# A new order for a list-scheduled kernel: the planner's table of priorities found anew with other costs for transfers and a few operations

## The chip, the core and the metric

The kernel runs on one core of a Trainium2 chip. Its engines are TensorE (PE, matrix products), VectorE (DVE), ScalarE (ACT), GpSimd (POOL) and SyncE (SP, which only issues transfers here). Each has a queue of its own and works through it in order; semaphores make one wait for another. The metric is the device time of one execution in microseconds, less is better.

## What is computed

Three layers one after the other, for 4 sequences of 576 tokens. Masks, scales and the subtraction of the maximum are as usual.

```python
# 1: attention, 8 heads of 64, each token sees itself and the 63 before it
scores = where(0 <= rel < 64, q @ k.T / 8, -1e9)
x = softmax(scores) @ v                              # heads side by side: 4 x 576 x 512
# 2: gated MLP over tokens
h = maximum(x @ w_in, 0)                             # 512 -> 1024
u, v = h[..., :512], h[..., 512:]
v_n = (v - mean(v)) / sqrt(var(v) + 1e-6)
v_s = einsum('ts,bsd->btd', w_spatial, v_n) + b_spatial[None, :, None]
y = (u * v_s) @ w_out
# 3: four causal attention heads of 64, each token's output is mixed from its top 2
logits = y @ w_gate
out = sum over e of gate_e * (softmax(causal(q_e @ k_e.T / 8)) @ v_e @ wo_e)
```

## The kernel before

Every product is made in three passes (high x high, high x low, low x high part of each number), so most operands exist as a pair of tiles with names in h and l: `xh, xl`, `vh, vl`, `wsp_h, wsp_l`, `woh, wol`, and weights as two tiles that both read `w`. Making a pair is a copy (`copy`, L432 on ACT, L434 on POOL, L436 on DVE) and a subtraction (`sub`, L445). Matmuls are issued by one helper (L421), transposes on PE at L688. In rows, `bank` is one of 8 PSUM banks.

Of the first layer, `a_couple` handles a pair of tiles of heads: the score products (`kt,qa`, 24 matmuls of 128 columns, called a score run here), the masked maximum on DVE (L654), the exponential on ACT (L660), the normalisation (`s_norm`, on ACT, DVE or POOL: L666, L669, L672), transposes on PE (`ident,pa`), the product with v (`pt,wol`), and then the pair `xh, xl`, and `xt` for the last 64 tokens. Of the second, `b_v` makes a v product for 128 tokens (`w,xh` and `w,xl`, 12 matmuls of 512 columns; the short one for the last 64 tokens reads `w,xt`), `b_u` a u product (`xh,w`, 12 of 288), `b_mix` the spatial product with its gate, and `prep64` unpacks and splits a weight that came by a load. w_out is multiplied into the weights of the third layer (`fold`, reading `w,woh`, 12 matmuls of 256). Of the third, `c_split` makes the pair of y for one of four column groups, `c_qk` and `c_v` are its products, `c_vt` that for the last 64 tokens of two sequences together (`w,zt`); `zeros` clears tiles (`pg`, L1107) that live from then on in the space that the second layer frees.

None of this runs in the order in which it is written. Each step is a node with the engines that may do it and a cost on each; the class `Planner` keeps, while the program is built, a clock of its own for each engine, and at each free engine starts the ready node with the lowest number in the table `KEY` (one number a node), given room in the ring of tiles that it needs. Scalars weigh in: `SWITCH` (the price of a change between kinds of matmul on PE), `DVE_BIAS`, `POOL_BIAS` and `EFT` (which of several possible engines takes a node), each with a value for each of two phases. The second phase begins with the third layer's tiles. `start` is where a node's end is worked out, with a model of the transfers that SP issues (`LAT`, `ISSUE`, `WAY`, `RATE`, `FLIGHT`, `BEHIND`). Costs and models change no instruction; they change the order and the engine. While operands are awaited at the start, up to 68 dummy products (`bank<-ident`, fillers) keep PE at work.

Of the kernel before, what the change touches and what calls it, by code (L numbers as in the profile page):

```python
# [14 lines left out]
ALU = mybir.AluOpType  # L15
# [14 lines left out]
SWITCH = (508440.848706, 3824.76008776)  # L30
A_BIAS = 10098.0
C_BIAS = 162315.0
DVE_BIAS = (1446.55002243, 3797.32105423)
POOL_BIAS = (791.503455194, 4900.20685501)
# [3 lines left out]
EFT = (590.178157957, 1602.10028593)  # L38
# [6 lines left out]
    1e+09, 1e+09, 1e+09, 1e+09, 1e+09, 1e+09, 1e+09, 1e+09, 1e+09, 1e+09, 1e+09, 1e+09, 1e+09, -1183064.921, -1180401.788, -984440.607, -770425.267, -965452.953, -700022.553, -767274.631, -735858.745, -731589.461, -769196.477, -803420.559,  # L45
# [132 lines left out]

class Planner:

    LAT = 200.0, 165.0, 130.0, 75.0, 900.0
    ISSUE, WAY, RATE, FLIGHT = 475.0, 650.0, 360.0, 8

    DRAIN = ((0.0, 138.0, 137.0, 191.0, 0.0),
             (212.0, 0.0, 158.0, 212.0, 165.0),
             (204.0, 151.0, 0.0, 204.0, 157.0),
             (194.0, 141.0, 140.0, 0.0, 147.0),  # L190
# [165 lines left out]
def attn_gmlp_moe_kernel(ctx: ExitStack, tc: tile.TileContext, kq0, qT, kT, v, w_in, wspT, b_sp, w_outT,  # L356
# [87 lines left out]
    def sub(e, o, a, hi):  # L444
        engs[e].tensor_tensor(out=o, in0=a, in1=hi.bitcast(F32), op=ALU.subtract)  # L445
# [1187 lines left out]
```

## Time and profile before

| | us |
|---|---|
| median of 3 runs | 417.92 |
| lowest and highest | 417.04, 418.19 |
| the profiled execution | 418.14 |
| its span in the trace | 416.4 |
| PE busy | 406.7 (98%) |
| DVE busy | 294.8 (71%) |
| ACT busy | 247.4 (59%) |
| POOL busy | 127.2 (31%) |

The span runs from the first to the last instruction in the trace; the execution's own time is 1.7 us longer. Busy times count each engine by itself, so they overlap. A line of the timeline gives when a group of like instructions starts, how long it lasts, engine and source line, output and inputs, their shape, how many there are, and in square brackets how long the engine was idle before and for whom it waited. Where matmuls follow one another, the next starts before the last has drained, so durations overlap a little.

### The profile page before, as it was taken

The page shows a single profiled execution, that of the slowest core. Times are in us where ns is not written, and L with a number is a line of the kernel's source. Part 1 is how long each engine was busy: PE and PEld are TensorE (multiplying, and loading weights), DVE is VectorE, ACT ScalarE, POOL GpSimd, SP SyncE. Part 2 cuts the span into 40 slices and gives each one's busy share as a digit, 9 for nine tenths or more (in the row PEclk, how much of TensorE's full clock was granted, in tenths as well). Part 3 has the DMA queues.
Part 4 walks back from the last instruction along what each step waited for, and adds up shares of the span by engine and source line. Part 5 has one row for each costly group of instructions (what it writes and reads, how often), then busy time and mean ns, then how long its engine had stood idle before and what let it go on. Part 6 is the DMA issues. An engine that isn't in the chain of part 4 may idle for free.

```text
span 416.4 us, 10959 instructions
## 1 busy us (share of the span) xinstructions
PE 406.7 (98%) x3854; PEld 368.3 (88%) x3854; DVE 294.8 (71%) x1213; ACT 247.4 (59%) x824; POOL 127.2 (31%) x191
## 2 busy tenths in 40 slices
PE   8997999999999999999999999999999999999996
PEld 8986799988899988999889999999979987988775
DVE  5989676988672777823552556499999899969640
ACT  4899799867591645911342343276565558547573
POOL 6227278333540136300310117044132114204110
PEclk9999699999999999999999999999999999999999
DMA  7996474979477664762100100014844865891833
GB/s 254 360 325 202 124 238 119 272 195 277 122 229 199 168 172 148 182 160 64 45 3 0 52 2 1 2 39 123 237 111 119 258 179 158 254 251 41 226 117 126
DMA packets 75625, 64.05 MB, mean 154 GB/s; under 512 B 12145, under 2 KB 69233, under 8 KB 75570
## 3 DMA queue, kind: packets, MB, share of 16 engines
q1 hardware_dynamic: 75570, 63.35, 52.7%
q8 instruction: 30, 0.49, 0.5%
q14 instruction: 25, 0.20, 0.2%
HBM read 43.15 MB, written 20.19 MB: 152 GB/s over the span
## 4 chain that ended last, share of the span: by engine, by line
PE 82%; DVE 6%; DMA 4%; ACT 3%; POOL 2%; issue 2%; SPq 1%; DVEq 0%; POOLq 0%; ACTq 0%
PE bank L421 80%; DMA y<-in_w_in_dram 1%; PE bank L1432 1%; DMA d<-p 1%; DVE pa L654 1%; DMA pg<-d 1%; DVE p L1403 1%; SPq L520 1%; PE bank L688 1%; ACT pa L660 1%; POOL xl L445 1%; ACT p L1353 0%; DVE p L1360 0%; ACT pa L666 0%; ACT xh L432 0%
## 5 line engine op out<-in xcount | busy, mean ns | idle before, releaser
L421 PE MATMUL bank<-xh,w 128*128 128x288 f32 x512 | 108.0, 297 | 0.0
L421 PEld LDWEIGHTS bank<-xh,w 128*128 128x128 f32 x512 | 83.7, 188 | 1.0 <-DVE mx L677 0.3
L421 PE MATMUL bank<-xl,w 128*128 128x288 f32 x256 | 75.4, 294 | 0.0
L421 PE MATMUL bank<-w,xh 128*128 128x512 f32 (+1 forms) x256 | 64.7, 343 | 0.0
L660 ACT ACTIVATE pa<-pa,mx 128x128 f32<-128x128 f32 x144 | 55.9, 397 | 4.3 <-DVE mx L654 4.2
L421 PEld LDWEIGHTS bank<-w,xh 128*128 128x128 f32 x256 | 44.0, 190 | 5.9 <-DVE mc L1355 0.4
L421 PEld LDWEIGHTS bank<-xl,w 128*128 128x128 f32 x256 | 48.1, 188 | 0.4
L1357 POOL TENSOR_SCALAR p<-p,mc,fx 128x256 f32<-128x256 f32 (+3 forms) x35 | 22.6, 652 | 79.7 <-DVE mc L1356 21.6
L421 PE MATMUL bank<-w,xl 128*128 128x512 f32 (+1 forms) x128 | 43.4, 339 | 0.0
L1353 ACT ACTIVATE p<-p,mc 128x128 f32<-128x128 f32 (+3 forms) x56 | 31.0, 557 | 15.4 <-DVE mc L1350 10.8
L421 PE MATMUL bank<-wsp_h,vh 128*128 128x288 f32 x128 | 37.9, 296 | 0.0
L421 PE MATMUL bank<-wsp_l,vh 128*128 128x288 f32 x128 | 37.7, 295 | 0.0
L421 PE MATMUL bank<-wsp_h,vl 128*128 128x288 f32 x128 | 37.7, 295 | 0.0
L654 DVE CUSTOM_DVE_ANT_0 pa<-bank,mask 128x128 f32<-128x128 f32 x120 | 28.6, 284 | 3.6 <-PE bank L421 3.6
L660 ACT ACTIVATION_READ_ACCUMULATOR pa<-pa,mx 128x1 f32 x144 | 28.2, 196 | 0.0
L900 POOL TENSOR_TENSOR st<-st,nhalf 128x1 f32<-128x1 f32 (+1 forms) x20 | 11.6, 582 | 52.0 <-DVE st L898 32.4
L432 ACT ACTIVATE xh<-bank 128x192 fp32r<-128x192 f32 (+1 forms) x35 | 12.5, 381 | 24.6 <-PE bank L421 24.4
L421 PEld LDWEIGHTS bank<-w,xl 128*128 128x128 f32 x128 | 24.2, 189 | 2.9
L1350 DVE CUSTOM_DVE_ANT_0 p<-bank,kmask 128x128 f32<-128x128 f32 (+3 forms) x56 | 25.6, 483 | 0.3
L666 ACT ACTIVATE pa<-pa,mx 128x128 f32<-128x128 f32 x69 | 22.5, 394 | 5.5 <-DVE mx L679 4.4
L965 DVE TENSOR_TENSOR y<-bank,ut 128x288 f32<-128x288 f32 x24 | 10.7, 450 | 21.2 <-PE bank L421 20.8
L421 PE MATMUL bank<-qk 64*128 64x288 f32 (+4 forms) x288 | 25.1, 319 | 0.1
(209 smaller groups left out, 985.5 us busy)
## 6 DMA issues: line engine op xcount, KB each, us to landing
vt<-in_v_dram SPq DMA_DIRECT2D x12, 512.0 KB, 5.4
dr<-pa SPq DMA_DIRECT2D x64, 96.0 KB, 2.3
pt<-dr SPq DMA_DIRECT2D x16, 384.0 KB, 4.1
d<-p SPq DMA_DIRECT2D x56, 96.0 KB, 2.5
qa<-in_qT_dram SPq DMA_DIRECT2D x44, 96.0 KB, 4.7
out_dram<-ot SPq DMA_DIRECT2D x15, 256.0 KB, 2.6
y<-in_w_in_dram SPq DMA_DIRECT2D x7, 512.0 KB, 6.7
d<-p SPq DMA_DIRECT2D x28, 128.0 KB, 2.6
```

The source lines that it names most:

```text
L421: pe.matmul(o, lhsT, rhs, start=start, stop=stop)
L432: act.activation(o, i, AF.Copy)
L445: engs[e].tensor_tensor(out=o, in0=a, in1=hi.bitcast(F32), op=ALU.subtract)
L520: nc.sync.dma_start(o, i)
L654: dve.tensor_tensor_reduce(out=at(j, e2), in0=sq(ps[:, j * 128:(j + 1) * 128]), in1=sq(mask(j)), scale=-0.125, scalar=3.0e38, op0=ALU.add, ...
L660: act.activation(at(j, e2), at(j, e2), AF.Exp, bias=mx[:, j, 0:1], scale=-1.0, accum_out=mx[:, j, 1:2])
L666: act.activation(at(j, e2), at(j, e2), AF.Copy, scale=mx[:, j, 3:4])
L900: a = N((POOL, 464), lambda e: pool.tensor_tensor(out=st[:m, 9:10], in0=st[:m, 8:9], in1=nhalf[:m], op=ALU.pow), [n1], use=[st])
L965: dve.tensor_tensor(out=o, in0=ps[:, :HS], in1=u[:, d, tk], op=ALU.mult)
L1350: a = N((DVE, t_tt(L)), lambda _, ps=ps, c0=c0, L=L, put=put, as4=as4, mc=mc, I=I: dve.tensor_tensor_reduce(out=put(), in0=as4(ps[:, c0:c0 ...
L1353: a = N((ACT, 284 + 0.87 * L), lambda _, put=put, mc=mc: act.activation(put(), put(), AF.Exp, bias=mc[:, 0:1], scale=-1.0, accum_out=mc[:, ...
L1357: done.append(N({POOL: 328 + 0.832 * L, DVE: 190 + 0.52 * L}, lambda en, put=put, mc=mc, fx=fx, I=I, ev=ev: engs[en].tensor_scalar(put(), ...
```

## The change

The same 2,024 nodes with the same dependencies are planned with another table and other numbers. All of `KEY` is new, of which one line stands here for all; of the costs, those on other engines stay.

```diff
-SWITCH = (508440.848706, 3824.76008776)
+SWITCH = (1103.82509147, 4097.35301413)
-DVE_BIAS = (1446.55002243, 3797.32105423)
-POOL_BIAS = (791.503455194, 4900.20685501)
+DVE_BIAS = (187.21718001, 3949.44476313)
+POOL_BIAS = (18.1796804764, 4795.43078564)
-EFT = (590.178157957, 1602.10028593)
+EFT = (5.94291314584, 2314.92076478)
 KEY = (
...
-    -785633.996, -981836.036, -983402.88, -1160481.899, -1201011.588, -786966.88, -991960.652, -1192566.939, -753919.869, -795775.002, -1192759.222, -701456.182, -700023.463, -1116725.173, -701789.343, -734601.776, -779059.107, -767422.523, -1183065.907, -778227.935, -1175730.814, -1188824.548, -969950.128, -961789.648,
+    -16078.292, -22240.116, -67920.549, -289169.335, -2246.71, 27470.204, -173567.753, -35079.124, 6051.637, -63771.512, -22257.935, 27662.349, -284945.631, -43488.426, -18625.122, 35208.97, -3805.54, 28877.627, -66786.575, -20726.325, -55124.883, 28023.696, -282775.152, 6423.47,
...
-    LAT = 200.0, 165.0, 130.0, 75.0, 900.0
-    ISSUE, WAY, RATE, FLIGHT = 475.0, 650.0, 360.0, 8
+    LAT = 200.0, 165.0, 130.0, 75.0, 300.0
+    ISSUE, WAY, RATE, FLIGHT = 475.0, 700.0, 335.0, 8
-    CLASH, BEHIND = 1.0, 2200.0
+    CLASH, BEHIND = 1.0, 1700.0
...
+        if e == PE and t - self.free[e] > 1500.0:
+            self.cold = t + 3400.0
         self.free[e] = n.end = t + n.on[e]
         if e == PE:
-            self.free[e] = n.end = n.end + self.DRAIN[self.form][n.form]
+            self.free[e] = n.end = n.end + self.DRAIN[self.form][n.form] + min(n.on[e], max(0.0, self.cold - t))
...
-                t = max(t, self.moved[-self.FLIGHT] + self.LAT[SP]) + self.ISSUE
-                behind = self.BEHIND if self.moved[-1] > t + self.WAY else 0.0
-                self.moved.append(max(self.moved[-1], t + self.WAY) + n.late / k / self.RATE)
-            self.free[e], n.end = t, self.moved[-1] + behind
+                t = max(t, self.moved[-self.FLIGHT] + 60.0) + self.ISSUE
+                self.data = max(self.data, t + self.WAY) + n.late / k / self.RATE
+                self.moved.append(self.data + 250.0 + min(self.BEHIND, 1.2 * (self.data - t - self.WAY)))
+            self.free[e], n.end = t, self.moved[-1]
...
-            a = N({POOL: 1053, DVE: 450, ACT: 880}, s_norm, [a], use=[pa, mx], prio=prio, sbuf=True)
+            a = N({POOL: 850, DVE: 450, ACT: 880}, s_norm, [a], use=[pa, mx], prio=prio, sbuf=True)
-        return N({POOL: 1225, DVE: 602}, lambda e: sub(e, lv(), a_(), hv()), [n5], use=[tmp, h, l], prio=prio, sbuf=True)
+        return N({POOL: 1300, DVE: 602}, lambda e: sub(e, lv(), a_(), hv()), [n5], use=[tmp, h, l], prio=prio, sbuf=True)
```

In the same way these costs change: POOL's of the sign step of `prep64` 588 to 640, of the split of w_spatial 1360 to 1480, of the power in the layer norm 464 to 560, of its scaling 850 to 780, of its split 1225 to 1300; DVE's of the two transposes 870 to 902 and 68 to 100 plus 4.16 a column.

What comes of it in the order: some 140 of the nodes go to another engine; ACT has 412 nodes after 455, DVE 899 after 853, POOL 152 after 155, PE 370 in both. Line numbers of the new program are 2 higher from L421 on.

The first place is PE between the score runs of the first sequence and its first u product. Names: `kt,qa` is a score run (its other rows are left out), `ident,pa` a set of three transposes, `pt,wol` a product with v, `w,xh 128x512` the first row of a v product, `w,xt` of the short v product, `xh,w` of a u product. Before:

```order
L421 MATMUL bank_73<-kt,qa 64x128
...
L688 MATMUL bank_75<-ident,pa 128x128 x3
L688 MATMUL bank_70<-ident,pa 128x128 x3
L421 MATMUL bank_74<-kt,qa 64x128
...
L421 MATMUL bank_73<-pt,wol 64x64 x12
L421 MATMUL bank_75<-kt,qa 64x128
...
L421 MATMUL bank_68<-w,xh 128x512 x2
...
L421 MATMUL bank_69<-w,xh 128x512 x2
...
L421 MATMUL bank_72<-w,xh 128x512 x2
...
L688 MATMUL bank_68<-ident,pa 128x128 x3
L421 MATMUL bank_73<-xh,w 128x288
```

Now:

```order
L423 MATMUL bank_68<-kt,qa 64x128
...
L423 MATMUL bank_75<-w,xh 128x512 x2
...
L423 MATMUL bank_69<-w,xh 128x512 x2
...
L690 MATMUL bank_74<-ident,pa 128x128 x3
L423 MATMUL bank_73<-kt,qa 64x128
...
L690 MATMUL bank_72<-ident,pa 128x128 x3
L423 MATMUL bank_75<-kt,qa 64x128
...
L423 MATMUL bank_69<-kt,qa 64x128
...
L423 MATMUL bank_74<-pt,wol 64x64 x12
...
L423 MATMUL bank_74<-w,xh 128x512 x2
...
L423 MATMUL bank_72<-w,xt 128x512
...
L423 MATMUL bank_74<-xh,w 128x288
```

Two of the three v products now stand ahead of two sets of transposes and the score runs; a third score run, a further set of transposes (the two sets around the last full v product are left out) and the short v product stand ahead of the first u product, and were behind it.

The second place is POOL at the change of stage, from the clearing of `pg` on. `y` is the layer's input for a column group pair, `zt` the operand of `c_vt`. Before:

```order
L1107 MEMSET pg_3517 64x4x32 x2
L434 TENSOR_SCALAR xh<-y_1256 128x576 x2
L445 TENSOR_TENSOR xl<-y_1256,xh 128x576 x2
L434 TENSOR_SCALAR zt_3536<-xh 128x64
L434 TENSOR_SCALAR zt_3537<-xl 128x64
L434 TENSOR_SCALAR zt_3536<-y_1256 128x2x64
L445 TENSOR_TENSOR zt_3537<-y_1256,zt_3536 128x2x64
L434 TENSOR_SCALAR zt_3536<-y_1296 128x2x64
L445 TENSOR_TENSOR zt_3537<-y_1296,zt_3536 128x2x64
```

Now:

```order
L1109 MEMSET pg_3482 64x4x32 x2
L436 TENSOR_SCALAR xh<-y_1342 128x576 x2
L447 TENSOR_TENSOR xl<-y_1342,xh 128x576 x2
L436 TENSOR_SCALAR zt_3502<-xh 128x64
L436 TENSOR_SCALAR zt_3503<-xl 128x64
L436 TENSOR_SCALAR zt_3502<-y_1307 128x2x64
L436 TENSOR_SCALAR zt_3502<-y_1342 128x2x64
L447 TENSOR_TENSOR zt_3503<-y_1307,zt_3502 128x2x64
L447 TENSOR_TENSOR zt_3503<-y_1342,zt_3502 128x2x64
L436 TENSOR_SCALAR zt_3502<-xh 128x64 x2
L436 TENSOR_SCALAR zt_3503<-xl 128x64 x2
```

Behind the last row stand two more pieces of `zt` for the second column group; in the order before, two of the twelve pieces are on ACT.

The third place is PE at the same moment, from the end of the last mix (`t2w,t2v`) on; `w,woh` is the first row of a fold, `w,zt` of `c_vt`, `w,xh 128x260` of a `c_v`, `xh,w` of a `c_qk`. Before:

```order
L421 MATMUL bank_70<-t2w,t2v 128x288
L421 MATMUL bank_71<-w_3409,woh 128x256
...
L421 MATMUL bank_75<-w_3409,woh 128x256
...
L421 MATMUL bank_68<-w_3409,woh 128x256
...
L421 MATMUL bank_73<-w,xh 128x260 x2
...
L421 MATMUL bank_74<-w,zt_3536 128x260 x2
```

Now:

```order
L423 MATMUL bank_69<-t2w,t2v 128x288
L423 MATMUL bank_70<-w_3369,woh 128x256
...
L423 MATMUL bank_68<-w_3369,woh 128x256
...
L423 MATMUL bank_73<-w_3369,woh 128x256
...
L423 MATMUL bank_72<-w,zt_3502 128x260 x2
...
L423 MATMUL bank_71<-xh,w 128x288
...
L423 MATMUL bank_74<-w,xh 128x260 x2
```

The product on `zt` now stands right behind the folds, where one on `xh` stood.

## Rows read from the trace of the kernel before

**Rows 1.** The page: busy time by engine, and the granted clock in 40 slices.

```profile
PE 406.7 (98%) x3854; PEld 368.3 (88%) x3854; DVE 294.8 (71%) x1213; ACT 247.4 (59%) x824; POOL 127.2 (31%) x191
...
PEclk9999699999999999999999999999999999999999
```

**Rows 2.** Waits of PE: total us, times, longest.

```profile
PE bank L421 <- issue: 1.8, 1, 1.8
...
PE bank L688 <- POOL pa L672: 1.4, 1, 1.4
```

**Rows 3.** By stretch: length, busy us of PE, PEld, DVE, ACT, POOL; clock, DMA share, GB/s.

```profile
38.51:42.59 4.08, 0.89 (x9) 0.67 (x7) 4.08 (x31) 4.08 (x21) 2.71 (x4) 0.93 0.73 190
42.59:48.90 6.31, 6.31 (x76) 5.24 (x77) 3.21 (x14) 3.46 (x16) 1.36 (x3) 0.51 0.27 85
```

**Rows 4.** Timeline of PE, 37 to 64 us: start, duration, then as described above.

```profile
37.63 0.89 PE L421 MATMUL bank<-kt,qa 64*64 64x128 f32 x24
...
42.59 1.68 PE L421 MATMUL bank<-kt,qa 64*64 64x128 f32 x24 [1.75 <-issue]
...
47.16 1.22 PE L421 MATMUL bank<-w,xh 128*128 128x512 f32 x2
...
50.81 0.62 PE L421 MATMUL bank<-w,xh 128*128 128x512 f32 x2
...
56.37 0.49 PE L688 MATMUL bank<-ident,pa 128*128 128x128 f32 x3
56.62 0.38 PE L421 MATMUL bank<-xh,w 128*128 128x288 f32 x1
56.83 0.29 PE L421 MATMUL bank<-xl,w 128*128 128x288 f32 x1
...
63.39 2.01 PE L421 MATMUL bank<-w,xt 128*128 128x512 f32 x8
```

**Rows 5.** By stretch, columns as in rows 3; DVE is the third busy time.

```profile
5.90:31.64 25.74, 25.74 (x341) 23.29 (x341) 23.12 (x110) 23.53 (x92) 8.78 (x18) 1.00 1.05 341
5.90:49.09 43.19, 39.83 (x557) 34.77 (x557) 36.41 (x188) 38.06 (x157) 18.23 (x29) 0.92 0.84 266
```

**Rows 6.** Waits of DVE between 5.9 and 57 us.

```profile
DVE pa L654 <- PE bank L421: 3.4, 2, 3.1
DVE xl L445 <- ACT xh L432: 3.0, 2, 2.7
```

**Rows 7.** Timeline of POOL from 248.7 us.

```profile
248.72 0.93 POOL L1107 MEMSET pg<- 64x128 f32 x4 [7.77 <-PE bank L421]
249.63 1.31 POOL L434 TENSOR_SCALAR xh<-y 128x576 fp32r<-128x576 f32 x2
250.90 2.83 POOL L445 TENSOR_TENSOR xl<-y,xh 128x576 fp32r<-128x576 f32 x2
253.70 0.51 POOL L434 TENSOR_SCALAR zt<-xh 128x64 fp32r<-128x64 f32 x1
254.18 0.24 POOL L434 TENSOR_SCALAR zt<-xl 128x64 fp32r<-128x64 f32 x1
...
254.59 0.29 POOL L434 TENSOR_SCALAR zt<-y 128x128 fp32r<-128x128 f32 x1
...
255.06 0.45 POOL L445 TENSOR_TENSOR zt<-y,zt 128x128 fp32r<-128x128 f32 x1
```

**Rows 8.** Timeline of PE from 248.7 us.

```profile
248.71 0.40 PE L421 MATMUL bank<-w,woh 128*128 128x256 f32 x2
...
253.02 0.41 PE L421 MATMUL bank<-w,xh 128*128 128x260 f32 x2
...
254.94 2.27 PE L421 MATMUL bank<-w,zt 128*128 128x260 f32 x12 [0.31 <-POOL zt L434]
```

**Rows 9.** Timeline of DVE, 246 to 254 us.

```profile
246.70 0.46 DVE L445 TENSOR_TENSOR xl<-pa,xh 128x288 fp32r<-128x288 f32 x1 [0.51 <-ACT xh L432]
...
249.95 4.17 DVE L445 TENSOR_TENSOR xl<-pa,xh 128x288 fp32r<-128x288 f32 x1 [0.51 <-ACT xh L432]
```

More of the change, by code (lines that the diff above doesn't have):

```diff
@@ L44 @@
     1e+09, 1e+09, 1e+09, 1e+09, 1e+09, 1e+09, 1e+09, 1e+09, 1e+09, 1e+09, 1e+09, 1e+09, 1e+09, 1e+09, 1e+09, 1e+09, 1e+09, 1e+09, 1e+09, 1e+09, 1e+09, 1e+09, 1e+09, 1e+09,
-    1e+09, 1e+09, 1e+09, 1e+09, 1e+09, 1e+09, 1e+09, 1e+09, 1e+09, 1e+09, 1e+09, 1e+09, 1e+09, -1183064.921, -1180401.788, -984440.607, -770425.267, -965452.953, -700022.553, -767274.631, -735858.745, -731589.461, -769196.477, -803420.559,
[82 rows of a table removed]
+    1e+09, 1e+09, 1e+09, 1e+09, 1e+09, 1e+09, 1e+09, 1e+09, 1e+09, 1e+09, 1e+09, 1e+09, 1e+09, -295605.994, -144360.526, -49680.67, -22256.667, -39347.276, 27469.015, -18107.127, -22875.689, -18692.581, -18626.594, -26031.425,
[82 rows of a table added]
 )
@@ L191 @@
              (0.0, 145.0, 144.0, 198.0, 0.0))
-    CLASH, BEHIND = 1.0, 2200.0
+    CLASH, BEHIND = 1.0, 1700.0
     def __init__(self):
         self.nodes, self.free, self.prio = [], [1500.0, 2000.0, 2900.0, 7600.0, 560.0], 0.0
-        self.moved, self.unit = [-1e9] * self.FLIGHT, 0
+        self.moved, self.data, self.cold, self.unit = [-1e9] * self.FLIGHT, 0.0, 0.0, 0
         self.phase = self.form = self.asked = 0
@@ L694, in a_couple @@
         if far:
-            a = N((DVE, 870), lambda e: dve.transpose(pa.t, pa.t), done, use=[pa], prio=prio, sbuf=True)
+            a = N((DVE, 902), lambda e: dve.transpose(pa.t, pa.t), done, use=[pa], prio=prio, sbuf=True)
             dr = r_dr.new()
@@ L821, in prep64 @@
         else:
-            n2 = N({POOL: 588, DVE: 335}, sign, [n0], alloc=[tmp], use=[raw], prio=prio, sbuf=True)
+            n2 = N({POOL: 640, DVE: 335}, sign, [n0], alloc=[tmp], use=[raw], prio=prio, sbuf=True)
             n3 = N((DVE, 602), lambda e: dve.scalar_tensor_tensor(p_().bitcast(I32), word(0), 29, p_().bitcast(I32),
@@ L842, in prep_sp @@
                    use=[raw], prio=prio, sbuf=True)
-            n2 = N({POOL: 1360, DVE: 670}, lambda e, x=x, k=k: sub(
+            n2 = N({POOL: 1480, DVE: 670}, lambda e, x=x, k=k: sub(
                 e, wsp_l[:, k, :], raw[:, x, :], wsp_h[:, k, :]), [n1], use=[raw], prio=prio, sbuf=True)
@@ L899, in b_v @@
         n2 = N((DVE, 70), lambda e: dve.tensor_scalar(st[:m, 10:11], st[:m, 6:7], -1.0, None, op0=ALU.mult), [a], use=[st])
-        a = N((POOL, 464), lambda e: pool.tensor_tensor(out=st[:m, 9:10], in0=st[:m, 8:9], in1=nhalf[:m], op=ALU.pow),
+        a = N((POOL, 560), lambda e: pool.tensor_tensor(out=st[:m, 9:10], in0=st[:m, 8:9], in1=nhalf[:m], op=ALU.pow),
               [n1], use=[st])
-        a = N({DVE: 460, POOL: 850}, lambda e: engs[e].tensor_scalar(
+        a = N({DVE: 460, POOL: 780}, lambda e: engs[e].tensor_scalar(
             vr[:m], vr[:m], st[:m, 10:11], st[:m, 9:10], op0=ALU.add, op1=ALU.mult), [a, n2], use=[vr, st], sbuf=True)
@@ L907, in b_v @@
             a = N(on_copy(512, 1, False), lambda e: copy(e, vh.t, vr.t), [a], alloc=[vh], use=[vr], sbuf=True)
-            a = N({POOL: 1225, DVE: 602}, lambda e: sub(e, vl.t, vr.t, vh.t), [a], alloc=[vl], use=[vr, vh], sbuf=True)
+            a = N({POOL: 1300, DVE: 602}, lambda e: sub(e, vl.t, vr.t, vh.t), [a], alloc=[vl], use=[vr, vh], sbuf=True)
         else:
@@ L1359, in far @@
                     use=[P, mc, fx], prio=prio, sbuf=True))
-        a = N((DVE, 68 + 4.16 * w), lambda e: dve.transpose(P[:, :4 * w], P[:, :4 * w]), done, use=[P], prio=prio, sbuf=True)
+        a = N((DVE, 100 + 4.16 * w), lambda e: dve.transpose(P[:, :4 * w], P[:, :4 * w]), done, use=[P], prio=prio, sbuf=True)
         d2, grp = r_d2.new(), int(tiles[0] > 1)
```

162 rows, old and new, of the table KEY are left out of this document.

## The prediction

> **What bounds the kernel now.** I began with the page: share of each engine and the clock line [rows 1]. The reader is to see two things there. TensorE (PE) is busy 406.7 of 416.4 us, and no other engine is near that. The one dip in the row of the granted clock is in the fifth slice, near 42 to 52 us. So, with the same matmuls in both programs (370 pieces of PE work, 3,854 instructions), the new order can gain only where PE waits, works at its lower clock, or fills time with dummy matmuls.
>
> Next, PE's own waits [rows 2]: two of them, 1.75 (1.8 in the list) and 1.4 us, lie close together. The table by stretch [rows 3] and PE's timeline [rows 4] show what they do. From 38.51 to 42.59 us PE works 0.89 us in all and waits 3.2; from 42.59 to 48.90 it is always busy but granted 0.51, so 1.2 GHz of its 2.4. A run of 24 score matmuls takes 1.68 us in that stretch and 0.89 just before it. The work of those 6.31 us would take 3.2 us at the full clock: 3.1 us lost, besides 3.2 us of waits. The second wait ends at 42.59; its releaser reads "issue", so nothing that the profile names, but the score run there is the first user of a kt tile that comes by a load.
>
> Third, DVE, whose products PE uses at the start. It is busy 23.12 of 25.74 us up to 31.64 and 36.41 of 43.19 up to 49.09 [rows 5]. Of the 6.8 us that it is idle up to then, most hang on PE's slow stretch (3.4 us waiting for a PSUM bank, 3.0 us for a copy of one; both sums of the stretch to 57 us) [rows 6]. DVE nearly saturated, then, sets when operands are ready.
>
> Fourth, the change of stage near 249 to 257 us, where POOL alone works through a string of small operations [rows 7], PE's product on zt waits for pieces of it [rows 8], and DVE is held up [rows 9].
>
> **Part 1, the start.** In the new order two v products (PE rows with w,xh) are put right behind the score run of 37.63, ahead of the transposes and the score run that waited for kt. A v product takes 2.78 us at the full clock (12 matmuls; the two that start at 50.81 and 53.59 end at 56.37) and 3.65 in the slow stretch (47.16 to 50.81) [rows 4]. Two are 5.6 us of work in the hole of 38.5 to 42.6. They need an xl that before made at 31.64, and DVE has more to do ahead of it: 20 pieces are moved in front (9.7 us at the durations that they have in before), 3 behind (1.7 us). So 23.1 + 8.0 = 31.1 us of DVE work, done at 37.0 with no idle time and at 40.5 with before's share of 23.12/25.74. I take 39: the hole is then filled but for half a microsecond, and kt is there, as in before by 42.59, when its run comes at 44.6.
>
> The next limit is the weight split that the first u product needs (before: w<-y,w on DVE at 49.09). Ahead of it stood 36.4 us of DVE work; 32 pieces come in front (12.9 us) and 7 go behind (2.5), so 46.8, and 0.7 for itself. Never idle, it is done at 5.9 + 47.5 = 53.4; at the share up to 31.64 at 58.8. In before the first u product starts at 56.62. In the new order PE has by then also done one more score run (0.89 us), one more set of transposes (0.25 from start to start) and the short v product on xt (2.01) [rows 4]: less 0.1 where they overlap, 3.05 us of work more. With the split done at 53.4 PE itself cannot be there before 55.0 (a v product whose operand has 43.5 us of DVE work ahead of it, so not before 49.7, the transposes, the short product and what else stands between), and the gain is 56.6 + 3.05 − 55.0 = 4.6; with 58.8 it is 0.8. I take 3.0, a little above the middle, since most of DVE's idle time hung on the PE waits that go. No fillers are saved or added: 68 in both, 61 of them ahead of the first v product.
>
> Over the whole program ACT loses 26 us of work at before's durations and DVE gets 14, all before the change of stage. From 57 us on PE's own work covers that, and I cost it at nothing; if the cover goes, what DVE is late shows as waits of PE there, for which the spread between the ends above (3.8 us) leaves room.
>
> **Part 2, the change of stage.** With S for the end of the last mix product, PE does three folds (36 matmuls) until S + 4.31 (248.71 to 253.02, 0.12 a matmul) [rows 8]. Then before put a v product on xh, and zt after it; the new order puts the product on zt first. POOL cannot start before S in either program: the zeroing reuses space that the last mix frees. Its chain in rows: zeroing 0.91, two copies 1.27, two subtractions 2.80, so S + 4.98 when the first zt piece starts [rows 7]. In the new order all 12 zt pieces are on POOL (10 before, 2 on ACT), and the pieces of the second of the four column groups come last. They take 0.51 (the first), 0.24 (64 wide), 0.29 (128 wide) and 0.45 (subtraction), each less the 0.03 by which neighbours overlap (253.70 + 0.51 against 254.18) [rows 7]: the first matmul can start at S + 6.2, the last operand is there at S + 8.3, and seven matmuls of 0.12 us stand behind it: S + 9.2. Without a wait the product would end at 4.31 + 1.44 = 5.75. Lost: 3.4. Before's product on zt could have begun at 253.02 + 1.44 = 254.46, began at 254.94 and took 2.27 us for 1.6: 1.1 lost [rows 8]. The difference is +2.3, to +2.8 with a semaphore's delay for each piece; I take 2.5.
>
> The subtraction on DVE that takes 4.17 us there (0.46 for the same operation three microseconds earlier) [rows 9] costs nothing in either order: it ends before PE has use for it. The Trainium skill, page "SBUF — State Buffer", section "SBUF: two separate sides", says why such a row can be so long: DVE and GpSimd share a pair of ports as an exclusive lock, held for a whole instruction, when a DVE operation reads two SBUF inputs against a GpSimd one that reads SBUF; the trace agrees with its 4.17 us. By that rule a DVE subtraction that got the pair first could also push POOL's chain, and the product on zt with it, back by up to 0.46 us, which would make the sum 2.1 instead of 1.7; no row of before shows that side.
>
> **Part 3, the clock.** Two waits of 1.4 to 1.8 us within 4 us were followed by half the clock in before [rows 3]. The new order has a wait of 1.9 us at S + 4.3 and then works 1.4 of the next 3.0 us. At the start I find waits left, too (about 1.2 us near 47 and 2 near 50, where v operands come from DVE one at a time). Bounds for a fall at one of the two: 0 (the 1.1 us of the stage change in before had none: the clock row stays at 9 there [rows 1]) and 3.1 (the whole of before's slow stretch). At the stage change part of the slow stretch would lie under the wait for POOL, which leaves 1.5 to 3.1; I take 2.0.
>
> **Part 4, small things.** Runs of one kind of matmul: 127 after, 124 before. The first of a new run takes 0.38 where the next takes 0.29 [rows 4]: 3 x 0.09, so +0.2. Loads: by the bytes issued ahead of each, none falls later than its user; at nothing, with 0.5 either way. In the tail the last pieces are in another order but PE has no gap there in either, nothing.
>
> **The sum.** −3.0 + 2.5 + 2.0 + 0.2 = +1.7. The profiled run took 418.14 us (span 416.4 and 1.7 around it), so 419.8; the median of the runs is 0.2 below the profiled one, so **419.6**.
>
> **The rivals.**
> *Forecast*, 0.42: as summed, the clock falls at one of the two places. For it: the same pattern did it at 42. Slower by 0.4%.
> *The clock holds*, 0.32: nothing in Part 3, −0.3 in all, 417.6. For it: the one other wait of the kind in before, over 1 us at the stage change, left the clock alone; against it: the new wait is nearly twice as long, with idle gaps right behind it.
> *DVE never idles at the start*, 0.26, the case on the other side: DVE's queue is fed without a break since ACT has less to do, the full 4.6 us come in, and the stage change costs its lower 2.3, with no fall of the clock: −2.1, so 415.8. It decides where the weight split ends before 54.5 us. Against it: DVE was idle a tenth of the time even when PE never waited (up to 31.64).
> That the change does nothing can be left out: the order differs on every engine.
>
> **How the numbers follow.** The low end: 4.6 gained and only 1.5 lost at the stage change, 415.0. The high end: 0.8 gained, 2.8 + 0.3 lost, clock 2.0: 422.2. What lies outside (both worst ends with the full 3.1) I leave out. A difference under 0.3%, 1.25 us, is about what a measurement of this kernel cannot tell from none. The forecast and its range lie mostly above that, the second case within it, the third below: faster 0.26, same 0.32, slower 0.42.
>
> **What would show it.** Right: v products at 38 to 41 us and no row "issue" of 1.75; a first u product near 56 to 57 with the short v product ahead of it; the product on zt spread over 3 us with POOL zt as releaser; a stretch with clock 0.5 at one of the two places. Wrong: a stage change that costs under 1.5 us more than before, a first u product later than 59, or waits of over 1 us between 60 and 245 us, which I have costed at nothing.

## The result, and the profile after

The new order takes 423.15 us (median of 4 runs, 421.41 to 424.32) against 418.06 before (4 runs): ratio 1.0121, 95% interval 1.0074 to 1.0168. It is slower, by 5.1 us. Executions of one kernel differ in whether the granted clock falls: where it matters below, the mean of those with a mean granted clock of 0.999 or more ("full clock") is given apart from the mean of the others, each with their count in brackets. The profiled execution took 422.18 us, span 420.4, so 4.0 us more than that of before. Three milestones of PE split these 4.0 us; S is again the end of the last mix product.

| us | before | after | difference |
|---|---|---|---|
| first u product starts | 56.62 | 55.71 | −0.9 |
| S | 248.87 | 244.44 | −4.4 |
| from S to the third layer's first score product | 20.52 | 25.34 | +4.8 |
| from there to PE's last matmul | 143.74 | 147.39 | +3.6 |
| from there to the span's end | 3.2 | 3.2 | 0.0 |

The page of the new kernel (busy us, share, instructions; granted clock in 40 slices), which answers to [rows 1]:

```profile
PE 407.2 (97%) x3854; PEld 369.1 (88%) x3854; DVE 313.3 (75%) x1261; ACT 223.9 (53%) x745; POOL 125.0 (30%) x188
...
PEclk9999999999999999999999998999999999999999
```

The dip of the clock is no longer in the fifth slice but at the change of stage, near 252 us. The waits of PE (total us, times, longest), which answer to [rows 2]:

```profile
PE bank L423 <- POOL zt L436: 3.3, 2, 2.7
...
PE bank L690 <- DVE mx L656: 1.3, 1, 1.3
PE bank L423 <- DVE mc L1405: 1.1, 1, 1.1
PE bank L423 <- DVE mc L1421: 1.1, 1, 1.1
```

The wait of 1.75 us at the start has gone. One of 2.7 us stands at the change of stage, and two of 1.1 in the third layer, where before had none over 0.4.

**The start.** PE's timeline (start, duration, then as in [rows 4]):

```profile
37.84 0.73 PE L423 MATMUL bank<-w,xh 128*128 128x512 f32 x2
...
43.90 0.89 PE L423 MATMUL bank<-kt,qa 64*64 64x128 f32 x24
...
49.65 0.52 PE L690 MATMUL bank<-ident,pa 128*128 128x128 f32 x3 [1.35 <-DVE mx L656]
...
53.77 2.10 PE L423 MATMUL bank<-w,xt 128*128 128x512 f32 x8
...
55.71 0.29 PE L423 MATMUL bank<-xh,w 128*128 128x288 f32 x1
```

The v product fills the hole at 38, score runs take 0.89 throughout, and the short v product is done ahead of the first u product. By stretch, columns as in [rows 3], DVE the third busy time:

```profile
5.90:31.64 25.74, 25.74 (x338) 23.58 (x340) 25.21 (x111) 22.14 (x85) 10.79 (x20) 1.00 1.05 347
5.90:49.09 43.19, 41.76 (x600) 36.21 (x598) 41.54 (x203) 38.01 (x144) 22.04 (x33) 1.00 0.95 304
```

DVE is busy 41.54 of 43.19 us, 36.41 before [rows 5].

**The change of stage.** S is the end of the last row that reads `t2w,t2v`, in before and then after:

```profile
248.58 0.29 PE L421 MATMUL bank<-t2w,t2v 128*128 128x288 f32 x1
```

```profile
244.15 0.29 PE L423 MATMUL bank<-t2w,t2v 128*128 128x288 f32 x1
```

POOL, PE and DVE, which answer to [rows 7 to 9]:

```profile
244.29 0.92 POOL L1109 MEMSET pg<- 64x128 f32 x4 [9.30 <-PE bank L423]
245.20 1.54 POOL L436 TENSOR_SCALAR xh<-y 128x576 fp32r<-128x576 f32 x2
246.71 3.74 POOL L447 TENSOR_TENSOR xl<-y,xh 128x576 fp32r<-128x576 f32 x2
250.42 0.24 POOL L436 TENSOR_SCALAR zt<-xh 128x64 fp32r<-128x64 f32 x1
```

```profile
251.43 0.51 PE L423 MATMUL bank<-w,zt 128*128 128x260 f32 x2 [2.69 <-POOL zt L436]
252.27 0.39 PE L423 MATMUL bank<-w,zt 128*128 128x260 f32 x1 [0.33 <-POOL zt L447]
253.29 2.17 PE L423 MATMUL bank<-w,zt 128*128 128x260 f32 x9 [0.63 <-POOL zt L436]
255.26 0.45 PE L423 MATMUL bank<-xh,w 128*128 128x288 f32 x1
```

```profile
245.42 0.80 DVE L447 TENSOR_TENSOR xl<-pa,xh 128x288 fp32r<-128x288 f32 x1
246.13 1.68 DVE L447 TENSOR_TENSOR w<-vt,w 128x1024 fp32r<-128x1024 f32 x1
```

PE waits 2.69 us, gets its operands piece by piece, and works on at half the clock. The granted clock stands behind the five busy times, 0.87 and then 0.50:

```profile
252.00:254.00 2.00, 1.10 (x5) 0.90 (x6) 0.00 (x0) 0.00 (x0) 1.43 (x7) 0.87 0.00 0
254.00:256.00 2.00, 2.00 (x11) 2.00 (x11) 0.09 (x1) 0.50 (x3) 0.00 (x0) 0.50 0.00 0
```

POOL's two subtractions of 128x576 take 3.74 us; before's took 2.83 [rows 7]. The first of them alone takes 2.38 us, 1.43 in before: it starts at 246.71, while DVE's subtraction of 128x1024 (the split of the last weight) runs until 247.81.

**The third layer.** Its whole stretch, before and then after:

```profile
269.39:413.13 143.74, 142.97 (x1199) 124.95 (x1198) 118.35 (x512) 89.18 (x272) 36.51 (x49) 1.00 0.57 159
```

```profile
269.78:417.17 147.39, 144.97 (x1199) 127.04 (x1198) 121.00 (x508) 89.49 (x272) 36.09 (x49) 1.00 0.55 154
```

The same 1,199 matmuls take 3.6 us more. Taken step by step, from a step's start to the next one's, 3.4 of them lie on the 16 products with v and on the score runs that stand ahead of some of them. PE and SP (the queue that issues transfers: `d<-p` stores probabilities to DRAM, `pg<-d` loads them back in another layout) show two of these places:

```profile
312.16 2.29 PE L423 MATMUL bank<-pg,v 128*64 128x320 f32 x14 [1.05 <-DVE mc L1421]
...
346.33 2.38 PE L423 MATMUL bank<-pg,v 128*64 128x320 f32 x14 [1.08 <-DVE mc L1405]
```

```profile
299.62 2.66 SPq L522 DMA_DIRECT2D pg<-d  x3
302.33 2.20 SPq L522 DMA_DIRECT2D d<-p  x4
308.58 0.93 SPq L522 DMA_DIRECT2D pg<-d  x2
...
337.98 5.43 SPq L522 DMA_DIRECT2D d<-p  x8
343.58 2.29 SPq L522 DMA_DIRECT2D pg<-d  x4
```

SP in before, for the same loads:

```profile
302.04 2.40 SPq L520 DMA_DIRECT2D pg<-d  x3
...
340.15 2.32 SPq L520 DMA_DIRECT2D pg<-d  x4
```

Counted from the first score product, the last loads of the first place were issued by 35 us in before and at 38.8 to 39.7 now, those of the second at 70.8 to 73.1 and now 73.8 to 76.1, so some 3 to 4 us later. The products stand little later (40.8 and 42.4 us; both 76.5). At the first place the loads took 3.5 us to land, the first at 312.1 us, and the product starts at 312.16; at the second, 2.7 us, so 346.2, and the product starts at 346.33. At the first place the loads waited for the four stores ahead of them, which landed late behind loads of 512 KB (DMA issues, 300 to 313 us: KB each, median us to landing; after, then the stores in before):

```profile
pg<-d SPq DMA_DIRECT2D x2, 512.0 KB, 5.6
...
d<-p SPq DMA_DIRECT2D x4, 96.0 KB, 5.1
```

```profile
d<-p SPq DMA_DIRECT2D x4, 96.0 KB, 2.0
```

The releaser that the two rows of PE name is DVE's `mc`; the landings just ahead of each product say that it was the loads.

### The profile page after: what moved, and what is told of

Read it like the earlier page. It is cut to its first block, busy times and chain, and to the rows that moved or that the text cites. A ratio compares the mean times of both kernels' runs of the same rounds, so it can differ in the third digit from the quotient of the medians.

```text
span 420.4 us, 10955 instructions
## 1 busy us (share of the span) xinstructions
PE 407.2 (97%) x3854; PEld 369.1 (88%) x3854; DVE 313.3 (75%) x1261; ACT 223.9 (53%) x745; POOL 125.0 (30%) x188
## 5 line engine op out<-in xcount | busy, mean ns | idle before, releaser
L662 ACT ACTIVATE pa<-pa,mx 128x128 f32<-128x128 f32 x144 | 55.8, 392 | 6.9 <-DVE mx L656 6.8
L1359 POOL TENSOR_SCALAR p<-p,mc,fx 128x256 f32<-128x256 f32 (+3 forms) x34 | 21.2, 626 | 77.3 <-DVE mc L1358 32.5
L1355 ACT ACTIVATE p<-p,mc 128x256 f32<-128x256 f32 (+3 forms) x56 | 31.0, 556 | 18.0 <-DVE mc L1352 11.4
L671 POOL TENSOR_TENSOR pa<-pa,mx 128x384 f32<-128x384 f32 x18 | 16.9, 942 | 41.8 <-DVE mx L681 26.4
L423 PE MATMUL bank<-pg,v 128*64 128x128 f32 (+2 forms) x224 | 24.2, 353 | 2.1 <-DVE mc L1405 1.1
L1352 DVE CUSTOM_DVE_ANT_0 p<-bank,kmask 128x256 f32<-128x256 f32 (+3 forms) x56 | 25.4, 483 | 0.9 <-POOL p L1359 0.6
```

The source lines that it names most:

```text
L423: pe.matmul(o, lhsT, rhs, start=start, stop=stop)
L662: act.activation(at(j, e2), at(j, e2), AF.Exp, bias=mx[:, j, 0:1], scale=-1.0, accum_out=mx[:, j, 1:2])
L671: engs[e].tensor_tensor(out=o, in0=o, in1=mx[:, None, :, 3:4].to_broadcast([128, 4, 3, 32]), op=ALU.mult)
L1352: a = N((DVE, t_tt(L)), lambda _, ps=ps, c0=c0, L=L, put=put, as4=as4, mc=mc, I=I: dve.tensor_tensor_reduce(out=put(), in0=as4(ps[:, c0:c0 ...
L1355: a = N((ACT, 284 + 0.87 * L), lambda _, put=put, mc=mc: act.activation(put(), put(), AF.Exp, bias=mc[:, 0:1], scale=-1.0, accum_out=mc[:, ...
L1359: done.append(N({POOL: 328 + 0.832 * L, DVE: 190 + 0.52 * L}, lambda en, put=put, mc=mc, fx=fx, I=I, ev=ev: engs[en].tensor_scalar(put(), ...
```

## The experiments

All kernels below are the same program with the planner's choice replaced by a fixed list of nodes and engines, so that single nodes can be moved (their line numbers differ). The kernel before was run beside each of them, and each ratio is to it on the same chip; there its medians are 415.9 to 417.2 us (by chip 415.4 to 416.2 at full clock, 417.0 to 417.6 without). Letters in the quoted expectations name theories within that text.

### Which stage

The layers' orders were crossed: PE, DVE, ACT, POOL and SP follow one list up to the change of stage and the other behind it.

```diff
-list: new layers 1 and 2, new layer 3
+new1_old2: new layers 1 and 2, old layer 3
+old1_new2: old layers 1 and 2, new layer 3
```

> First two layers in the new order (1,114 nodes), third layer in the order of before (910 nodes), both as fixed lists, no planner. Theory A (the start gains, the change of stage and the third layer lose): the end of the last mix is 4.4 us earlier than in before, as in the new kernel, and everything behind it runs as in before, so 418.1 - 4.4 = 413.7 us. Rival B (the old order of the third layer only fits the state in which its own first part left the queues, so the gain is lost at the change of stage): 417 us or more.

> The reverse: first two layers in the order of before, third layer in the new order. Theory A: the 8.4 us that the new kernel loses behind the last mix appear whole, 418.1 + 8.4 = 426.5 us, 4.8 of them between the folds and the third product behind them, 3.6 later. Rival B (the new third layer suffers only from the first part of its own order): under 421 us.

Measured: new1_old2 417.14 us, ratio 1.0002 (0.9979 to 1.0026); old1_new2 422.51, ratio 1.0151 (1.0111 to 1.0191). The time is lost only with the new third layer, its change of stage included. The new start is worth little: at full clock new1_old2 took 415.07 (4) against 416.2 (16) before. Theory A's sizes were missed in both, since the change of stage does not belong to one list alone. From S to the first score product the four profiles have:

| us | old third layer | new third layer |
|---|---|---|
| old first layers | 20.52 | 23.06 |
| new first layers | 22.90 | 25.34 |

The new third layer adds 2.5 there, and the new first layers another 2.4, with either third layer. POOL's subtractions, in new1_old2 and in old1_new2, show what the first layers bring with them:

```profile
247.24 3.77 POOL L510 TENSOR_TENSOR xl<-y,xh 128x576 fp32r<-128x576 f32 x2
```

```profile
248.78 2.79 POOL L510 TENSOR_TENSOR xl<-y,xh 128x576 fp32r<-128x576 f32 x2
```

They are long with the new first layers, in whose order DVE splits the last weight beside them.

The new order as a list, with nothing moved, on the chip of the next runs:

> The new order itself, as a fixed list, so that the other three have it on the same chip. It should stand 5 us above before (ratio 1.012). The first runs left it open how much of the start's gain was luck of the clock: before's profiled run had half the clock from 42 to 49 us, while the same first part in the run with the old first layers and the new third layer kept the full clock there and reached the end of the last mix 2.1 us earlier.

Measured: 423.23 us, ratio 1.0156 (1.0126 to 1.0185). In its profile the clock falls at the start, too, in the same order that held it in the profile of after:

```profile
52.00:54.00 2.00, 2.00 (x6) 1.56 (x5) 2.00 (x8) 1.74 (x8) 0.65 (x1) 0.50 0.72 213
```

### The change of stage

```diff
 new_zt_third, PE (ACT's and DVE's copies behind these products likewise):
-product on zt, c_qk, c_v
+c_qk, c_v, product on zt
 new_zero_late, POOL:
-clearing of pg, xh xl of y (4 nodes), 12 pieces of zt
+xh xl of y (4 nodes), 12 pieces of zt, clearing of pg
 new_sub_early, DVE:
-last gate, ..., split of the last weight (w<-vt,w)
+split of the last weight (w<-vt,w), last gate, ...
```

> The new order with one move at the change of stage: the product on zt goes behind the first q/k product and the first v product of the third layer, with its copies behind theirs; POOL's queue is the same. Theory A (PE's wait for POOL's string is the loss there, 5.2 us of waits and 0.7 of low clock): PE waits about 1.2 us for the second split and about half a microsecond for the last zt piece, the three products end at S + 10.2 instead of S + 14.7, and the time is 423.2 - 4.5 = 418.7 us. Rival C (DVE bounds the third layer, so what is saved at its beginning is given back as waits of PE between 270 and 350 us): 421 us or more.

Measured: 417.05 us, ratio 1.0028 (1.0003 to 1.0053). By the ratios this is 1.3% less than the new order: what PE works on while POOL makes `zt` is worth over 5 us, the falls of the clock included. The time from S to the first score product is 20.83 us, 25.34 in after.

> The new order with the clearing of pg moved on POOL from the head of the third layer's queue to behind the twelve zt pieces; nothing else. Theory D (the planner starts POOL's string when POOL is free, some 9 us before POOL really starts, since it does not know that the clearing waits for the space that the last mix frees): the splits now run while the last mix is on, the zt pieces are done by about S + 4, the product on zt follows the folds without a wait, and 5.5 to 5.9 us come back: 423.2 - 5.7 = 417.5 us. Rival E (the splits and zt wait for the same release, whoever stands first): POOL still starts at S and ends 0.9 us earlier, 422.3 us.

Measured: 420.23 us, ratio 1.009 (1.006 to 1.0119). Its POOL:

```profile
236.05 1.72 POOL L499 TENSOR_SCALAR xh<-y 128x576 fp32r<-128x576 f32 x2
237.73 3.26 POOL L510 TENSOR_TENSOR xl<-y,xh 128x576 fp32r<-128x576 f32 x2
249.93 0.24 POOL L499 TENSOR_SCALAR zt<-xh 128x64 fp32r<-128x64 f32 x1 [8.94 <-PE bank L486]
```

The splits need nothing from the last mix: with the clearing behind them they began 9.5 us before S. Only the clearing waits for S, and it holds up POOL's queue (9.30 us idle in after). But `zt` itself starts at S + 4.4, since its tiles take space that the last fold releases. So only half of the cost comes back.

> The new order with one pair of operations moved: the copy and the subtraction that split the last third-layer weight (subtraction of 128x1024 on DVE, 1.68 us at 246.1 in the new kernel) go ahead of the last gate, so before POOL begins its splits. Theory G (DVE subtractions with two SBUF inputs and POOL's hold each other up, and this is why POOL's two subtractions took 3.74 us in the new kernel and 2.83 in before): POOL's two subtractions take 2.8 to 3.2 us, the product on zt starts 0.5 to 1.0 us earlier after the end of the last mix, 0.5 to 1 us of the total. Rival H (POOL's duration differs for another reason): 3.7 us as before and no change.

Measured: 419.86 us, ratio 1.0086 (1.0057 to 1.0115). POOL's subtractions:

```profile
247.14 2.80 POOL L510 TENSOR_TENSOR xl<-y,xh 128x576 fp32r<-128x576 f32 x2
```

With DVE's split of the last weight out of the way they took 2.80 instead of 3.74 us. That 0.9 us brought 2.9 us in the times, more than either theory gave; the wait is shorter, and the slow stretch behind it goes. The first score product comes 23.09 us behind S, as with the old first layers (23.06).

> The mixed kernel with six dummy products (0.22 us each) on PE in its wait of 1.4 us ahead of the set of transposes at 50.2 us, into the bank that these transposes then overwrite; they add work of 1.3 us that lies in the wait. Theory I (in about half the executions of the new first part PE falls to half the clock behind that wait, which makes the following v product 4.4 us instead of 2.9 and costs 2.2 us): the fall goes, the slower executions go, and the median is 0 to 1.1 us under the mixed kernel without them, its spread under 1.5 us. Rival J (the fall has nothing to do with that wait): the same spread and, if the dummies delay the transposes, up to 0.5 us more.

```diff
 # mixed_best (below), ahead of the transposes of pair 13
+for _ in range(6):
+    mm(ps2[:, :128], ident, ident)
```

Measured: 414.09 us, ratio 0.9933 (0.9906 to 0.9959), as mixed_best. It decides nothing: the dummies waited just as long as the work that they should bridge, since they write the same PSUM bank.

```profile
50.13 1.60 PE L486 MATMUL bank<-ident 128*128 128x128 f32 x12 [1.25 <-DVE mx L719]
```

### The third layer

```diff
 new_pv_later, PE (on new_zt_third):
-product with v 3, c_qk 16
+c_qk 16, product with v 3        # and likewise c_qk 24 ahead of products 7 and 5
 new_sp_moves, SP (on new_zt_third):
-load 11 (512 KB), stores 8      |  stores 14 (x4), loads 21 (x2)
+stores 8, load 11 (512 KB)      |  loads 21 (x2), stores 14 (x4)
 new_sp_first: the first of these two moves alone
```

> The new order with the product on zt third (as in the second experiment of that kind) and two moves in the third layer: one q/k product goes between the two products with v that start at 308.8 and 312.2 us in the new kernel, and one goes ahead of the product with v of 346.3 us, which itself stands a little later. Theory A2 (the 3.0 to 3.6 us that every run with the new third layer loses behind its first scores are waits of PE there for a bank or a load, 1.05 and 1.08 us, with nothing else to do): 2 us come back, so 415 us where the run with the product on zt third gave 417.1, and the stretch from the first scores to PE's end goes from 146.9 to 145 us. Rival F (DVE, over 90% busy there, is late for everything, so another product waits instead): under 0.7 us back.

Measured: 417.55 us, ratio 1.002 (0.9995 to 1.0046). In the profile the two waits went and the stretch from the first score product to PE's end fell to 145.88 us from 146.90, but an output product (`w,ot`) waited 0.6 us instead. The times moved by less than their interval.

> As new_zt_third, with SP's queue alone changed: four stores of one tile stand behind a 512 KB load of probabilities instead of... that is, the stores go ahead of that load, and at the second place two loads of probabilities go ahead of the four stores that stood before them. Theory K: the two waits of products with v in the third layer (1.06 and 0.74 us in new_zt_third) are loads that land just when the products could begin (309.71 and 343.38, products at 309.80 and 343.48); with both loads issued in time some 1.4 us come back: the stretch from the third layer's first scores to TensorE's end is 145.5 instead of 146.90 us, and the ratio to the kernel before falls from 1.0028 to 0.9995 or less. Rival F: something else is late at once in their place, and under 0.5 us comes back (stretch above 146.4, ratio 1.001 to 1.004).

Measured: 418.68 us, ratio 1.0036 (1.001 to 1.0063), stretch 148.26 us. The wait at the first place went; the second became worse. SP and PE there:

```profile
341.37 1.92 SPq L585 DMA_DIRECT2D d<-p  x4
345.01 0.93 SPq L585 DMA_DIRECT2D pg<-d  x2
```

```profile
347.59 2.43 PE L486 MATMUL bank<-pg,v 128*64 128x320 f32 x14 [1.75 <-DVE mc L1415]
```

The two loads at 345.01 read what the four stores ahead of them write, so they wait for those to land; I had delayed their own stores.

> As new_sp_moves, but with its first move alone: the four stores of one tile stand on SP behind a 512 KB load of probabilities that they stood ahead of in new_zt_third; at the second place the order of new_zt_third is kept. New_sp_moves lost the wait of 1.06 us at its first place and gained one of 1.75 us at its second, where loads came to wait for stores that had been put behind other loads. Theory K (late loads are a part of the third layer's loss): the wait at the first place stays away and nothing else takes its place, so the stretch from the third layer's first scores to TensorE's end is 145.7 to 146.0 us against 146.90, and the ratio to the kernel before falls from 1.0028 to about 1.000. Rival F: the time is lost again further on, the stretch stays above 146.5 us and the ratio at 1.002 or more.

Measured: 417.07 us, ratio 1.0026 (1.0006 to 1.0047). Its profile has no wait over 0.5 us for these products and a stretch of 145.13, better than theory K asked; the median is where it was, as rival F said. What an order waits for these loads differs between executions of the same order: the stretch was 146.90 in new_zt_third and 146.03 in its repeat. So one profile settles no more than the place. The next runs therefore take the suspected cause away for all products at once: new_no_roundtrip and old_no_roundtrip load an input in place of what the stores wrote, and new_no_stores leaves out the stores as well.

```diff
 new_no_roundtrip (on new_zt_third), old_no_roundtrip (on mixed_best):
-src = d2[:, :, :, :w].rearrange("i k a w -> (k a) i w")
+src = bass.AP(tensor=kT.tensor, offset=kT.offset, ap=[[256, 128], [32768, 4], [1, w]])
 new_no_stores (on new_no_roundtrip):
-for i in range(4):
-    dma(d2[i, :, :, :w]...., P[i * 32:(i + 1) * 32, :4 * w]....)
+pass
```

> New_zt_third once more, as the kernel that new_no_roundtrip is compared with on the same chip: ratio 1.003 to the kernel before, stretch 145.8 to 147.4 us by what its profiled execution waits for loads.

> As new_zt_third, but the loads of probabilities of the third layer (the half of them that goes through DRAM) read an input instead of what the stores before them wrote: same bytes, same shapes, same place in SP's queue, but they need not wait for those stores to land, nor does SP's queue behind them. The probabilities of those tiles are therefore not the kernel's own. Theory L (the third layer's loss is products with v that stand too early for loads that come through stores): the stretch from the third layer's first scores to TensorE's end falls from 146.9 to 143.6 to 144.4 us, and the ratio to the kernel before from 1.003 to about 0.996. Rival M (the loss is in the order of other work): the stretch stays above 145.5 and the ratio above 1.000.

> The same edit in mixed_best, which has the third layer of the kernel before. Theory L: there the loads come in time, so the stretch stays at 143.5 to 144.0 us and the ratio at 0.993. Rival M: if waiting for stores costs any order of this layer something, it falls here as well, by 0.5 us or more.

> As new_no_roundtrip (loads of the third layer's probabilities read an input), and the stores of these probabilities are left out as well, so that a load waits for no store to land and for none to be issued ahead of it on SP (in new_no_roundtrip eight stores at 334.44 took SP 5.17 us before four loads were issued at 339.65, and the product behind them waited 0.84 us). Theory Q (what is left of the third layer's loss is SP's queue): the waits of products with v go, the stretch from the third layer's first scores to TensorE's end falls from 145.6 to 143.6 to 144.4 us, and the ratio from 1.003 to 0.999 or less. Rival M (the loss is in the order of other work): the stretch stays at 145.0 or more and the ratio at 1.001 or more.

| | us | ratio | at full clock | without |
|---|---|---|---|---|
| new_zt_third_2 | 417.52 | 1.0034 (1.0009 to 1.0060) | 417.0 (9) | 419.5 (3) |
| new_no_roundtrip | 417.19 | 1.0029 (1.0010 to 1.0047) | 416.3 (6) | 418.1 (6) |
| new_no_stores | 416.73 | 0.9994 (0.9971 to 1.0018) | 415.5 (2) | 416.5 (10) |
| old_no_roundtrip | 413.28 | 0.9937 (0.9914 to 0.9960) | 413.1 (8) | 415.2 (4) |

The third layer's stretch in new_zt_third_2, new_no_roundtrip and new_no_stores:

```profile
265.38:411.41 146.03, 145.00 (x1199) 126.68 (x1198) 120.92 (x508) 89.41 (x272) 36.13 (x49) 1.00 0.55 156
```

```profile
267.94:413.56 145.62, 144.24 (x1199) 126.33 (x1198) 119.90 (x508) 89.50 (x272) 36.43 (x49) 1.00 0.56 156
```

```profile
267.28:410.99 143.71, 143.44 (x1199) 125.31 (x1198) 120.07 (x508) 89.33 (x272) 36.20 (x49) 1.00 0.25 76
```

That loads wait for their own stores to land is not the main thing. Without that wait the new third layer's median moves by less than its interval and its stretch stays at 145.62 (theory L gave 144.4 at most), and the old one does not change (stretch 143.97, 143.98 in mixed_best). At equal clock it gives 0.7 and 1.4 us, so a part of the loss may lie there. In new_no_roundtrip SP's queue still shows stores ahead of the loads, and PE behind them:

```profile
334.44 5.17 SPq L585 DMA_DIRECT2D d<-p  x8
339.65 2.14 SPq L585 DMA_DIRECT2D pg<-in_kT_dram  x4
```

```profile
342.53 2.42 PE L486 MATMUL bank<-pg,v 128*64 128x320 f32 x14 [0.84 <-DVE mc L1468]
```

With the stores left out as well the stretch is 143.71, that of before, and the ratio falls by 0.35% more; the two intervals just overlap, and the fall is found at either clock, at full clock with two executions only. The old third layer's stretch is 143.74 to 144.01 in all its profiles. So the third layer's loss is products with v that wait for loads held up on SP behind stores (theory Q). The old third layer without its stores was not run, so it is not shown that it would gain less; PE is idle 0.77 us in its stretch (143.74 less 142.97) and 0.27 in that of new_no_stores (143.71 less 143.44), so by these rows I estimate half a microsecond at most. What holds the loads most is not told apart: the issue of the stores, stores that wait for DVE's probabilities, or the bytes that they move (the DMA share falls from 0.56 to 0.25).

### A version that beats both

The old third layer with two moves at its head, behind the new first two layers (mixed_best) or behind the old ones (old_two_moves):

```diff
 PE:
-c_v, product on zt, c_v, c_qk
+c_v, c_v, c_qk, product on zt
 POOL:
-clearing of pg, xh xl of y, pieces of zt
+xh xl of y, pieces of zt, clearing of pg
```

> First two layers in the new order, third layer in the order of before, with two moves at the change of stage: POOL's clearing of pg behind the zt pieces (so that the splits run while the last mix is on), and the product on zt behind two v products and a q/k product. Theory A (what the run with the new first layers and the old third layer lost was PE's wait for POOL at the change of stage, 2.6 us more than in before): no wait there, PE's end 163.2 us after the last mix, 2.7 to 3.5 us under before. Rival B2 (the old third layer then waits elsewhere): within 1 us of before.

> The mixed kernel once more, beside the other two: 3.2 us under before (ratio 0.993).

> The order of before throughout, with the two moves of the mixed kernel at the change of stage (clearing behind the zt pieces, product on zt fourth). Theory A: before loses 1.1 us there, which comes back: 1 us under before, and the mixed kernel stays 2 us under this one, which is what the new first part is worth. Rival B3 (the mixed kernel's gain is all from the two moves): within 0.7 us of the mixed kernel.

Measured: mixed_best 413.58 us, ratio 0.9928 (0.9902 to 0.9954), and 414.19, 0.9924 (0.9899 to 0.9948), in its repeat; old_two_moves 414.66, 0.994 (0.992 to 0.996). The two moves work on the old order as well: `zt` is ready before PE comes to it. POOL in mixed_best:

```profile
249.35 0.24 POOL L499 TENSOR_SCALAR zt<-xh 128x64 fp32r<-128x64 f32 x1 [8.93 <-PE bank L486]
```

The first score product then starts 19.33 us behind S, 20.52 in before. In the medians most of the gain is the two moves, and the new first layers are worth 0.5 to 1.1 us. At full clock the two share it about evenly: before took 416.1 (13) on this chip, old_two_moves 414.7 (5), the mixed kernel 413.5 (5) and 413.2 (3).

## Why the prediction was right and wrong

The direction and the likeliest case were right (slower, with the clock falling at the change of stage); the size was not: +1.7 forecast, +4.0 between the profiles, +5.1 between the medians, and 423.15 lies above the range. The medians show more than the profiles because the profiled execution of after had a mean granted clock of 0.996, and the two slowest of its four (424.12 and 424.32 us) 0.987 and 0.992.

- **The start: right.** −3.0 forecast, −4.4 found, inside its bounds; v products at 37.84, first u product at 55.71, DVE nearer to never idle than I took it (96%, not 90). But 2.1 us of the 4.4 are chance: before's profiled execution was one in which the clock fell, and the same first layers without a fall reached S at 246.73 (old1_new2). The new start has such executions too (new_again). Like for like it is worth 0.5 to 1.5 us in the times.
- **The change of stage and the clock: right in sum, 2.5 + 2.0 forecast against 4.8 found, and in half of the mechanism.** The crossed orders give the new third layer alone 2.5 us (23.06 against 20.52), what Part 2 had for the product on zt put first. The other 2.4 us come with the new first layers, by a longer string on POOL and what follows from it; the fall of the clock, which Part 3 held to come of the wait as forecast, is only a part of it (`c_qk`, 1.58 us at full clock, took 2.32), and went with POOL's delay in new_sub_early. POOL's string was 1.15 us longer than its rows in before said. A DVE subtraction, too, ran longer beside it (0.80 against 0.46). I had allowed POOL's side 0.46 us, the length of a DVE subtraction of 128x288, and left it out of the sum; what stood beside POOL's first subtraction now was DVE's one of 128x1024, which ran until 247.81, and I had not followed where DVE would stand. That allowance came from the rule of the Trainium skill, page "SBUF — State Buffer", section "SBUF: two separate sides", by which the operation that starts first keeps the shared ports for its whole instruction; the trace (2.38 us in place of 1.43) and new_sub_early's 2.80 for both agree with it, and the instruction that I applied it to was the wrong one. That POOL cannot start before S is true of the clearing alone.
- **The step that failed: the third layer "at nothing".** Part 1 let PE's own work cover the third layer, and Part 4 said that no load falls later than its user, with 0.5 us either way. I compared bytes issued ahead of each load; I did not follow what a load stands behind on SP: the stores that it waits for, and the time that SP takes to issue them. It costs 3.6 us in the profile and 2 to 3.6 in every unaltered copy of that layer. Between the profiles this alone is more than the 2.3 us by which the forecast fell short; the start, 1.4 us better than forecast, hid a part of it. Without it the median would be near 419.5, inside the range. The text named "waits of over 1 us between 60 and 245 us" as a sign of being wrong; they came at 312 and 346, where it did not look.
- **The changes of kind (+0.2)** are too small to be told from this. The range's low end, 415.0, leaves out the 0.2 us by which the median lies under the profiled run (414.8 by its own sum); nothing hangs on it.
- **The rivals.** "The clock holds" was wrong in all eight executions of this order (mean granted clock 0.987 to 0.996 each, after and new_again). "DVE never idles" was nearly true in its premise (DVE's split of a weight at 53.18 ended at 53.83, ahead of the 54.5 that it named) and yet not in its result, since what follows took back more than the start could give.

## What to carry to other kernels

Where an order changes, check each load by its place in the issuing queue and by what the queue must issue and wait for ahead of it, not by its bytes. A stretch in which the bound engine "has no gap" in before says nothing of the order after. An instruction at the head of an in-order queue that waits for space (the clearing here) holds back work that could have run long before; put it behind that work, and put the consumer that is served piece by piece behind others that are ready. Where GpSimd works through a string that PE waits for, look up which DVE instruction the new order sets beside it. Compare executions at the same granted clock before a difference in milestones is credited to an edit.

## What was unexpected of the hardware

Two subtractions of 128x576 on POOL took 2.80, 2.83, 3.26 and 3.74 us in four orders; that DVE's work beside them decides it is shown for 3.74 against 2.80, by the one move of new_sub_early. Eight stores of probabilities kept SP's queue for 5.43 us in after and 5.17 in new_no_roundtrip, with four loads behind them; most took 0.3 to 0.5 us each, and one of the eight 1.91 and 1.66 us, for which the profile gives no reason. While POOL's string ran, one DVE subtraction of 128x288 stood for 4.17 us in before [rows 9] and for 6.25 in old1_new2, so over several of POOL's instructions and not one. And PE fell to 1.2 GHz at the start in one execution of an order and not in another, behind the same two waits (1.34 and 0.48 us both in new_zt_third, where it fell, and in its repeat, where it did not); what decides it stays open.
